# A convolution and attention kernel with its residual adds partly moved to accumulating DMAs, and its written-out orders made anew

## The chip, the cores and the metric

The kernel runs on one core of a Trainium2 chip. The metric is the time of one execution in microseconds of device time (us): lower is better. One execution of each kernel is also recorded by the hardware profiler; that gives the trace on which the readings rest. Five engines work side by side, each through its own instructions in order: TensorE (PE in the profile), VectorE (DVE), ScalarE (ACT), GpSimd (POOL) and SyncE (SP), which here only starts DMA transfers. They wait for one another through semaphores.

## The reference

The input is a residual stream x of 2048 tokens by 512 channels. Four layers run one after another: a long convolution, a local attention, the same convolution again, the same attention again, each on the layer-normalised stream and added back to it.

```python
def _A_ref(u, ...):                       # per channel d, states n = 0..127
    dt = jnp.exp(log_dt)[:, None]
    P = jnp.exp((dt * A)[:, :, None] * l[None, None, :])
    K = jnp.einsum("dn,dnl,dn->dl", Cc, P, dt * Bc).real      # kernel of 2048 taps
    y = irfft(rfft(u padded to 4096) * rfft(K padded))[:2048]
    return y + u * Dskip
def _B_ref(x, wqkv, wo):                  # 32 heads of 16, 8 taps, 2 tokens apart, causal
    q, k, v = (x @ wqkv) split
    logits = einsum(q, k at s, s-2, ..., s-14) / 4            # -1e9 ahead of token 0
    o = einsum(softmax(logits), v at the same tokens)
    return o @ wo
```

The convolution's kernel K is made once and used in both convolution layers.

## The kernel before

**Tiling.** The residual stream stays on the chip in one tile, X, 128 partitions by 16 "slots" of 512 channels in bfloat16: token 16p+j is in partition p, slot j. A slot is one 128x512 piece, and what follows in the attention is done by slot or by groups of four or eight slots.

**Stages.** There are five plans. The first makes the tables for K; the second finishes K (on PE, with sums evacuated by ScalarE or VectorE) and runs the first convolution as a two-step transform by matmuls; the third is the first attention (function b_layer), the fourth the second convolution (a_layer), the fifth the second attention. In the trace of before they end at about 60, 198, 308, 359 and 469 us.

**The order.** A layer's function doesn't issue its instructions directly. It puts operations on a list by `pl.op(engine, us, fn, *after)`, and where an operation can be done in several ways it puts all of them there with `pl.either(name, *ways)`. `Plan.run` then issues the operations in the order of one string of numbers per plan, ORDERS, which was written out by a planner offline; of a choice, those operations are issued whose numbers are in the string. `moved` (L317) is such a choice between a copy by ScalarE and one by VectorE. So a new ORDERS string can change both which engine does a step and what stands ahead of it on that engine. An engine runs its own instructions in this order whatever the others do; SP starts its transfers in it too, and if one must wait, all behind it wait.

**One attention**, with the lines named below:

- Statistics of the normalisation per slot (L166, VectorE), roots by Ln and Exp on ScalarE (L1401, L1402). The reciprocal deviations rs are needed for the earlier tokens too, which for some slots are one partition down: `shifted` (L1409), a small DMA from rs to rs by SP after a memset of partition 0 by POOL (L1420). Then rr, the products of the deviations of two tokens (L1422, VectorE), spread by ScalarE to RR (L1413), and ones written by POOL where no earlier token exists (L1419).
- Queries and keys by PE (L1436), evacuated to qT and kT by ScalarE or VectorE (L1441); the first columns of kT, shifted by a position, are filled by an SP transfer (L1446). Values into VX (L1456, L1467), with transfers that shift them (L1480).
- Logits: products on VectorE (L1501, 128x4096 or 128x2048), summed over a head's 16 channels on PE (L1512), copied back and turned (L1530, L1538, L1543), scaled by RR (L1581), masked by POOL (L1588).
- Softmax on 128x1024 tiles: a tree of maxima (L1562, VectorE), the maximum subtracted (L1624, VectorE), Exp (L1625, ScalarE); the sum either on PE (L1618) with Ln and Exp on ScalarE (L1599, L1603), or as a tree with a reciprocal on VectorE (L1593); the multiplication with it (L1627).
- Values: products on VectorE (L1640: 4096 columns, and 1024 or 512 in the last part), summed on PE (L1656, L1661) into po, evacuated by ScalarE (L1674, or L1676 straight into oT), and turned by an SP transposing transfer (L1679) into oT.
- The output projection of a slot: four matmuls by PE (L1719). Then the residual add in one of three ways: PE adds X by a matmul with the identity and ScalarE copies to X; or VectorE adds ps_o to X from PSUM (L1694); or ScalarE copies ps_o to oT (L1700) and VectorE adds oT to X (L1703). In the last attention the slot is then stored by SP (L1855).

The function `pv` (from L1630) builds the value part; `softmax`, just ahead of it, the subtraction and the sum; `out` the projection and the residual.

Of the kernel before, what the change touches and what calls it, by code (L numbers as in the profile page):

```python
# [10 lines left out]
ACT = mybir.ActivationFunctionType  # L11
# [33 lines left out]
STASH = ()  # L45

# [43 lines left out]
def make_consts(nc, const, C):  # L90
# [5 lines left out]
    for name in ("F1", "F1T"):  # L96
        C[name + "_h"] = nc.inline_tensor(_bf(fc[name]), name="c_" + name)
    todo = [("ident", _bf(np.eye(128)), BF), ("C2", _bf(fc["C2"]), BF), ("IC", _bf(fc["IC"]), BF),
            ("onesr", _bf(np.ones((1, 128))), BF)]
# [98 lines left out]
def load_params(nc, pp, prm):  # L198
# [1690 lines left out]
```

## Time and profile before

| what | value |
|---|---|
| median of 3 runs | 471.32 us (470.4 to 473.38) |
| profiled execution | 470.71 us, of which the traced span is 468.9 |
| granted TensorE clock | 0.999 |
| VectorE busy | 440.1 us (94%), 587 instructions |
| PE busy | 397.3 us (85%), 5255 matmuls |
| ScalarE busy | 347.1 us (74%) |
| POOL busy | 15.1 us (3%) |
| DMA | 49.34 MB in 110955 packets |
| DMAs started by POOL | none |

The span is the time from the first to the last traced instruction; the profiled execution's own time has some 1.8 us around it. Busy time counts an engine's instructions as the profiler saw them. A group of instructions is shown as line, engine, operation, tile written <- tiles read, shape, count, then busy time and mean duration (ns), then the time that the engine was idle just before them and what ended that. Durations of VectorE overlap a little with the next instruction's, so that the next starts some 0.07 us before the record's end.

### The profile page before, as it was taken

Reading aid. Unit: us, or ns where it says so; the run is one execution under the profiler, and the core shown is the slowest. Engines: PE = TensorE matmul, PEld = TensorE weight load, DVE = VectorE, ACT = ScalarE, POOL = GpSimd, SP = SyncE. Lnnn points to the kernel's source line nnn. Section 1 sums busy time; section 2 is a strip of 40 time slices with the busy share of each in tenths; the row PEclk is TensorE's granted clock in tenths of the full one; section 3 lists DMA queues with packets and bytes.
Section 4 is the critical chain, followed back from the end, with each engine's and each line's share of the span. In section 5 each row is a group of like instructions: output and inputs, shape, how many; then the busy total and the mean of one; then the engine's idle time right before and its main releaser. Section 6 shows DMA issues by size and latency. Waiting matters only on the chain. (4 is left out here: it accounts for less than half of the span.)

```text
span 468.9 us, 12383 instructions
## 1 busy us (share of the span) xinstructions
PE 397.3 (85%) x5255; PEld 244.0 (52%) x5255; DVE 440.1 (94%) x587; ACT 347.1 (74%) x546; POOL 15.1 (3%) x86
## 2 busy tenths in 40 slices
PE   1520688877999999899999979979998999998896
PEld 1410454544767768644466434666676445563353
DVE  6999999999999998589899999999996999999996
ACT  4999878895898878566786458999994668673341
POOL 0000000000000005000100000000000000100000
PEclk9999999999999999999999999999999999999999
DMA  8990036468379498521013221379937201113254
GB/s 234 189 344 22 3 93 140 56 102 173 103 139 202 78 150 175 139 49 62 36 46 106 51 45 30 91 223 182 194 73 98 49 7 49 60 46 78 46 135 113
DMA packets 110955, 49.34 MB, mean 105 GB/s; under 512 B 89019, under 2 KB 104124, under 8 KB 110644
## 3 DMA queue, kind: packets, MB, share of 16 engines
q1 hardware_dynamic: 110468, 48.16, 47.3%
q8 instruction: 41, 0.67, 0.6%
q10 hardware_dynamic: 432, 0.39, 0.3%
q14 instruction: 14, 0.11, 0.1%
HBM read 15.78 MB, written 8.13 MB: 51 GB/s over the span
## 5 line engine op out<-in xcount | busy, mean ns | idle before, releaser
L1640 DVE TENSOR_TENSOR prod<-VX,L 128x512 bf16<-128x512 bf16 (+2 forms) x72 | 75.7, 1101 | 0.3
L1501 DVE TENSOR_TENSOR prod<-qT,kT 128x4096 bf16<-128x4096 bf16 (+1 forms) x40 | 72.0, 1859 | 3.3 <-ACT kT L1441 2.9
L1436 PE MATMUL ps_qk<-U,wqk 128*128 128x512 bf16 x256 | 58.3, 379 | 1.7 <-ACT U L1361 1.1
L1656 PE MATMUL po<-prod,sb_ident 128*128 128x512 bf16 x224 | 52.4, 379 | 3.8 <-DVE prod L1640 3.6
L1436 PEld LDWEIGHTS <-wqk 128*128 128x128 bf16 x256 | 24.3, 97 | 33.8 <-issue 6.9
L1656 PEld LDWEIGHTS <-sb_ident 128*128 128x128 bf16 x224 | 21.6, 98 | 29.6 <-DVE prod L1640 3.6
L448 PE MATMUL ps_sum<-Ttab,sb_ident 128*128 128x512 bf16 x40 | 16.1, 403 | 19.9 <-DVE Ttab L409 19.2
L1719 PE MATMUL ps_o<-wo_t,oT 128*128 128x512 bf16 x128 | 32.7, 379 | 0.0
L865 ACT CAST Z<-ps_s 128x1024 bf16<-128x1024 f32 (+1 forms) x32 | 29.2, 978 | 4.2 <-PE ps_s L860 2.7
L1456 PE MATMUL ps_v<-wv,U 128*128 128x256 bf16 x256 | 31.6, 272 | 0.6 <-ACT VX L1467 0.3
L1467 ACT ACTIVATE VX<-ps_v,rs 128x256 bf16<-128x256 f32 x64 | 26.3, 473 | 5.6 <-PE ps_v L1456 5.0
L1456 PEld LDWEIGHTS <-U 128*128 128x128 bf16 x256 | 24.6, 97 | 8.4 <-issue 2.8
L473 DVE TENSOR_TENSOR Ttab<-Ttab,MPA 128x2048 bf16<-128x2048 bf16 (+2 forms) x20 | 28.1, 1429 | 0.0
L166 DVE BATCH_NORM_STATS2 ln_st_a<-X 128x6 f32<-128x512 bf16 x40 | 24.8, 680 | 3.1 <-ACT X L1001 2.9
L473 DVE TENSOR_TENSOR Y2tab<-Ttab,MPB 128x6144 bf16<-128x6144 bf16 (+1 forms) x13 | 27.2, 2120 | 0.0
L486 PE MATMUL psk<-Ttab 128*32 128x64 bf16 x1024 | 21.6, 201 | 4.0 <-DVE Ttab L473 4.0
L1674 ACT CAST ot<-po 128x1024 bf16<-128x1024 f32 x14 | 13.9, 1010 | 14.7 <-PE po L1656 11.7
L1441 ACT CAST kT<-ps_qk 128x512 bf16<-128x512 f32 x32 | 18.7, 584 | 7.6 <-PE ps_qk L1436 7.6
L489 PE MATMUL psk<-Y2tab,Ttab 128*32 128x48 bf16 x1024 | 21.2, 195 | 2.7 <-DVE Y2tab L473 1.7
L486 PEld LDWEIGHTS <-Ttab 128*32 128x32 bf16 x1024 | 19.3, 99 | 8.0 <-issue 7.0
L1441 ACT CAST qT<-ps_qk 128x512 bf16<-128x512 f32 x29 | 16.9, 587 | 8.3 <-PE ps_qk L1436 8.0
L453 ACT CAST Ttab<-ps_sum 128x1024 bf16<-128x1024 f32 (+1 forms) x24 | 20.5, 903 | 3.4 <-PE ps_sum L449 3.3
(233 smaller groups left out, 987.4 us busy)
## 6 DMA issues: line engine op xcount, KB each, us to landing
kt_scratch<-sp_k SPq DMA_DIRECT2D x16, 256.0 KB, 3.9
Kt<-kt_scratch SPq DMA_DIRECT2D x16, 256.0 KB, 5.3
X<-in_A_u_dram SPq DMA_DIRECT2D x8, 256.0 KB, 5.0
X<-in_A_u_dram SPq DMA_DIRECT2D x4, 512.0 KB, 5.0
out_dram<-X SPq DMA_DIRECT2D x16, 128.0 KB, 1.8
k_scratch<-KTq SPq DMA_DIRECT2D x7, 256.0 KB, 3.2
KT<-k_scratch SPq DMA_DIRECT2D x7, 256.0 KB, 3.9
VX<-VX SPq DMA_DIRECT2D x4, 448.0 KB, 3.7
```

The costliest lines, as they stand in the source:

```text
L166: self.nc.vector.bn_stats(self.st[:, j, part, :], X[:, :, j, a // 2:b // 2])
L473: nc.vector.tensor_tensor(d, src.to_broadcast([128, c, n, 2 * EYB]), mm, ALU.mult)
L486: nc.tensor.matmul(o.rearrange("e (s i) -> e s i", s=2), xs, T[:, 1:3, h, m // 2, :, t], start=(m == 0), stop=False, skip_group_check=True)
L865: nc.scalar.copy(box["Z", kind, dc][:, 0:n // 8, :, jq * 32:(jq + 1) * 32].rearrange("p g r k -> p r g k"), box.pop(("s1", kind, dc, jq))[ ...
L1436: nc.tensor.matmul(ps[:], wqk[:, ct, f0:f0 + 128], XT[:, ct // 2, 4 * s:4 * s + 4, ct % 2, :], start=(ct == 0), stop=(ct == 3))
L1441: copy((qT, kT)[which][fp][:, f2, o:o + 512], box.pop(("qk", which, fp, f2, s))[:])
L1456: nc.tensor.matmul(ps[:, jj].rearrange("p t h d -> p (t h d)"), XT[:, ct // 2, j + jj, ct % 2, :], wv[:, ct, fp * 256:(fp + 1) * 256], sta ...
L1467: nc.scalar.activation(out, ps, ACT.Identity, scale=r)
L1501: nc.vector.tensor_tensor(pr[:], windows(q, 0, 2), windows(kT[fp][:, a:a + n2, col(w):col(w) + 1024], -DIL * 128, 2), ALU.mult)
L1640: nc.vector.tensor_tensor(p2[:].rearrange("p w j t d h -> p w (j t) d h"), windows(v, -DIL * 256, taps), l.to_broadcast([128, taps, nj * 2 ...
L1656: nc.tensor.matmul(po[:, c:c + 512], ident[:], p2[:, t, k + j:k + j + 2].rearrange("p j t d h -> p (j t d h)"), start=first, stop=stop)
L1719: nc.tensor.matmul(ps, oT[:, ft // 2, o:o + 128], wo_t[:, ft, :], start=(ft == 0 and not res), stop=(ft == 3))
```

## The change

1. *Residual by DMA.* `out` gets a fourth way: ScalarE copies ps_o to oT (L1700 before), and POOL starts a DMA that reads oT and adds it to X where it lands. The new order takes it in the second attention for slots 0, 2, 3, 5 and 6.
2. *Shift by matmul.* `by_tensor` takes the place of the memset and the DMA of rs in both attentions: a float32 matmul with a shifted identity, `down`, into PSUM, and a copy (by ScalarE, in the new orders).
3. *Subtraction of the maximum by PE*, as another way: two matmuls add the logits and the negated maximum (with `minus`, the negated identity) in PSUM, and ScalarE takes Exp from there in two halves. The new order takes it once, in the second attention.
4. *Other ways of the last values*: `pv` is split into `pv` and `piece`, which offers five ways to evacuate and turn the values of slots 12 to 15. In the new orders the way taken is the one of the kernel before.
5. *More ways of smaller steps*: the extension of kT by a copy on ScalarE or VectorE instead of a DMA (taken once each in the first attention); statistics from sums of squares, `by_moments` (not taken).
6. *Constants*: `minus` (32 KB) and `down` (64 KB) are loaded in the first stage; two tiles, Drow and spread, move to a pool that is released later on.
7. *All five ORDERS strings are new.* Besides the above, some evacuations change engine. In the second plan three table sums and several evacuations move to VectorE and others to ScalarE, and some turns change between PE and DMA. In the second convolution some evacuations swap engines. In the second attention one softmax sum goes from PE and ScalarE to VectorE's tree with reciprocal, slots 1 and 7 go from adding out of PSUM to copying and adding, slot 13 the other way.

```diff
+SHIFT = True
-    todo = [("ident", _bf(np.eye(128)), BF), ("C2", ...
+    todo = [("ident", _bf(np.eye(128)), BF), ("minus", _bf(-np.eye(128)), BF), ("C2", ...
+            ("onesr", ...), ("down", np.eye(128, k=1, dtype=np.float32), F32)]
...
-            o = pl.op("G", 0.1, lambda: nc.gpsimd.memset(rs[0:1, 0:NV], 1.0))
-            o = pl.op("S", 0.5, shifted, o, *Rs.values(), lag=2.3)
+            def by_tensor():
+                def mm():
+                    ps = box["down"] = psA.tile([128, NV], F32, name="ps_down", tag="psA")
+                    nc.tensor.matmul(ps[:], C["down"][:], rs[:, NJ:NV + NJ], start=True, stop=True)
+                key = ("psA", "down")
+                return moved(pl, nc, ("down",), 0.2, 0.15, lambda copy: copy(rs[:, 0:NV], box.pop("down")[:]),
+                             pl.op("P", 0.2, mm, *Rs.values(), take=key), drop=key)
+            o = by_tensor() if SHIFT else by_dma()
...
-                Kx[fp, f2] = pl.op("S", 0.8, lambda: nc.sync.dma_start(...), Kd[fp, f2, 2], Kd[fp, f2, 3], lag=2.5)
+                Kx[fp, f2] = pl.either(("ahead", fp, f2), lambda: pl.op("S", 0.8, ahead(nc.sync.dma_start), ends, lag=2.5),
+                                       lambda: pl.op("A", 0.65, ahead(nc.scalar.copy), ends),
+                                       lambda: pl.op("V", 0.5, ahead(nc.vector.tensor_copy), ends))
...
+            def less_by_tensor(o):
...
+                        nc.tensor.matmul(ps[:], ident[:], Lf[:, ws], start=True, stop=False)
+                        nc.tensor.matmul(ps[:], C["minus"][:], x[2][:, 0, :].unsqueeze(1).to_broadcast([128, 4, 128]), start=False, stop=True)
...
+                        nc.scalar.activation(Lf[:, ws], box.pop(("less", h))[:], ACT.Exp, scale=DH ** -0.5)
...
+            o = pl.either(("less", fp, j0), lambda: less_by_vector(o), lambda: less_by_tensor(o))
...
+        def summed_taken(j):
+            nc.gpsimd.dma_start(X[:, :, j, :], spent(j), accum_op=ALU.add)
...
                     if res is None:
                         a = pl.op("A", 0.48, lambda: taken(j, box.pop(("o", j))[:]), a, drop=key)
+                        if slow:
+                            return pl.op("G", 1.2, lambda: summed_taken(j), a, lag=3.5)
                         return pl.op("V", 0.33, lambda: added_taken(j), a)
...
-                es.append(pl.either(("out", j), *ways[::-1] if qt in ADD_Q else ways, lambda: way(None)) if qt in VSTAT_Q else way(True))
+                es.append(pl.either(("out", j), *ways[::-1] if qt in ADD_Q else ways, lambda: way(None), lambda: way(None, True)) if qt in VSTAT_Q else way(True))
```

The numbers in `pl.op` are the planner's own figures for an operation; `Plan.run` doesn't use them.

More of the change, by code (lines that the diff above doesn't have):

```diff
@@ L1394, in by_sums, with by_moments, power, spread @@
                 return pl.op("A", 0.5, root, a)
+            def by_moments():
+                def power(j):
+                    nc.scalar.activation(halves(oT[:, j // 8, j % 8 * D:j % 8 * D + D]), X[:, :, j, :], ACT.Square, accum_out=rs[:, NV + j:NV + j + 1])
+                def spread():
+                    nc.vector.tensor_tensor(ln.mv[:, js, 0], nm[:, js], nm[:, js], ALU.mult)
+                    nc.vector.scalar_tensor_tensor(rs[:, NV + j0:NV + j1], rs[:, NV + j0:NV + j1], 1.0 / D, ln.mv[:, js, 0], ALU.mult, ALU.subtract)
+                def rooted():
+                    r = rs[:, NV + j0:NV + j1]
+                    nc.scalar.activation(nm[:, js], r, ACT.Ln, bias=eps[:, 0:1])
+                    nc.scalar.activation(r, nm[:, js], ACT.Exp, scale=-0.5)
+                key = ("psA", "sum", q)
+                a = pl.op("P", 0.9, sums, turned[q], Wd.get("k", []), take=key)
+                a = pl.op("V", 0.1, lambda: nc.vector.tensor_copy(nm[:, js], box.pop(("sum", q))[:]), a, drop=key)
+                b = [pl.op("A", 0.72, lambda j=j: power(j), ready) for j in range(j0, j1)]
+                return pl.op("A", 0.5, rooted, pl.op("V", 0.3, spread, a, b))
             def by_stats():
@@ L1630, in pv, with way, piece @@
         def pv(fp, j0, nj):
-            flat, np, taps = fp == 0 or j0 < 12, min(nj, 4), 2 if nj == 8 else 1
+            if nj > 2:
+                vs, last = piece(fp, j0, nj, True, None)
+            else:
+                before, vs, last = box["pv"], [], []
+                def way(flat, how):
+                    box["pv"] = before
+                    v, x = piece(fp, j0, nj, flat, how)
+                    vs.append(v)
+                    last.append(x)
+                    return Od[fp, j0]
+                o = pl.either(("piece", j0), lambda: way(False, "A"), lambda: way(False, "V"), lambda: way(True, "D"),
+                              lambda: way(True, "A"), lambda: way(True, "V"))
+                for k in range(j0, j0 + nj):
+                    Od[fp, k] = o
+            Od["last", fp, j0], box["pv"] = last, vs
+        def piece(fp, j0, nj, flat, how):
+            np, taps = min(nj, 4), 2 if nj == 8 else 1
             def part(w, first):
@@ L1678, in turn, with turn_mm, turn_back @@
             def turn(j):
-                nc.sync.dma_start(oT[:, fp, j * 256:(j + 4) * 256].rearrange("f (b p) -> f b p", p=128),
-                                  box.pop(("ot", fp, j))[:], transpose=True)
+                nc.sync.dma_start(oT[:, fp, j * 256:(j + np) * 256].rearrange("f (b p) -> f b p", p=128),
+                                  box.pop(("ot", fp, j))[:, 0:np * 256], transpose=True)
+            def turn_mm(j):
+                ot = box.pop(("ot", fp, j))
+                pt = box["pt", fp, j] = psO.tile([128, 4, 128], BF, name="pt_o", tag="psO")
+                for x in range(4):
+                    nc.tensor.transpose(pt[:, x, :], ot[:, x * 128:x * 128 + 128], ident[:])
+            def turn_back(copy, j):
+                copy(oT[:, fp, j * 256:(j + np) * 256].rearrange("f (b p) -> f b p", p=128), box.pop(("pt", fp, j))[:])
             os, vs = [], []
@@ L1719, in mm, with way @@
                         nc.tensor.matmul(ps, oT[:, ft // 2, o:o + 128], wo_t[:, ft, :], start=(ft == 0 and not res), stop=(ft == 3))
-                def way(res, j=j, key=key, mm=mm):
+                def way(res, slow=False, j=j, key=key, mm=mm):
                     if qt == 3:
```

52 lines of the change are left out of this document (37 added, 15 removed), and 120 rows, old and new, of the table ORDERS.

## The prediction

> **What bounds the kernel now.** I began with the page's busy totals, then cut the span into the five plans with the table by windows, and read three more views in the stages that the change touches: VectorE's waits, its groups of instructions, and the chain that ended last. The totals and the first stretch-by-stretch table:
>
> ```profile
> PE 397.3 (85%) x5255; PEld 244.0 (52%) x5255; DVE 440.1 (94%) x587; ACT 347.1 (74%) x546; POOL 15.1 (3%) x86
> ...
> 0.00:60.00 60.00, 22.10 (x588) 15.93 (x591) 54.51 (x97) 52.20 (x83) 0.90 (x11) 1.00 0.60 155
> 60.00:195.00 135.00, 120.28 (x2759) 83.00 (x2747) 130.38 (x146) 110.54 (x137) 7.47 (x13) 1.00 0.67 133
> 195.00:305.00 110.00, 104.03 (x739) 55.83 (x739) 103.77 (x140) 77.46 (x159) 3.35 (x31) 1.00 0.23 57
> 305.00:360.00 55.00, 50.90 (x505) 37.58 (x503) 48.06 (x78) 48.32 (x60) 0.10 (x1) 1.00 0.76 156
> 360.00:469.00 109.00, 100.02 (x690) 51.65 (x687) 103.41 (x130) 58.59 (x111) 3.31 (x30) 0.99 0.30 66
> ```
>
> Each row is a window: its length, then busy time of PE, weight loads, VectorE (DVE), ScalarE (ACT) and POOL, the granted clock, DMA. VectorE is filled in four of the five rows; only from 305 to 360, the second convolution, does PE lead (between 320 and 359 it is busy 37.82 of 39, VectorE 33.24). So a microsecond of VectorE in either attention should be worth nearly one, a microsecond of it in the second convolution little. VectorE's 26 us of idle time lie at the borders of stages:
>
> ```profile
> DVE prod L1501 <- ACT kT L1441: 2.9, 3, 1.3
> DVE ln_st_a L166 <- ACT X L1001: 2.9, 1, 2.9
> DVE X L1287 <- PE ps_y L1282: 2.7, 2, 1.4
> DVE pa L950 <- ACT sp_k L1059: 2.4, 2, 1.9
> DVE X L1694 <- PE ps_o L1719: 1.5, 5, 0.5
> ```
>
> (total, times, longest). The first attention begins with 1.33 us of waiting at 209.94 and 1.20 at 233.78 for keys that ScalarE had yet to evacuate; from 359 to the end VectorE almost never waits. The last part of the chain shows what ends the program:
>
> ```profile
> 442.12 2.21 DVE prod L1640
> 444.33 0.04 issue
> 444.38 1.89 PE po L1656 x8
> ...
> 462.79 2.60 PE ps_o L1719 x12
> 465.39 0.02 issue
> 465.41 0.69 DVE X L1694
> ```
>
> Up to 444.3 the chain is VectorE's products, and behind the last 4096-column product PE alone has 21.0 us without a hole. VectorE in the same stretch has 20.3 busy of 22. So here both must get shorter for the end to move.
>
> **The change, part by part.** The planned orders of the two kernels differ in which way each choice takes; I counted these per plan and priced them from the groups of the second attention:
>
> ```profile
> L1640 DVE TENSOR_TENSOR prod<-VX,L 128x4096 bf16<-128x4096 bf16 x12 | 27.1, 2287 | 0.0
> ...
> L1694 DVE TENSOR_TENSOR X<-ps_o,X 128x512 bf16<-128x512 f32 x11 | 7.6, 689 | 1.6 <-PE ps_o L1719 1.5
> ...
> L1624 DVE TENSOR_TENSOR L<-L,sm_m 128x1024 bf16<-128x1024 bf16 x4 | 2.8, 689 | 0.1
> ...
> L1703 DVE TENSOR_TENSOR X<-oT,X 128x512 bf16<-128x512 bf16 x5 | 2.1, 419 | 0.0
> ```
>
> (the last numbers: busy us, mean ns, idle before.) *Second attention.* Five residual adds go from VectorE to POOL's DMA: slots 0 and 3 save 2×0.69, slots 2, 5 and 6 save 3×0.42, 2.64 in all. Slots 1 and 7 become copy plus cheap add (−2×0.27), slot 13 the reverse (+0.27): −0.27. One subtraction of the maximum goes to PE (−0.69). Against that, one softmax denominator leaves PE and ScalarE for VectorE: a tree by L1562 (0.42+0.29+0.29) and a reciprocal like L1593's 0.95; by start-to-start pitch, a little under these durations, +1.63. The small rest: one key copy fewer net (−0.61). The sum is −2.6 by durations, and about −2.1 when each is counted by the pitch at which VectorE starts the next (some 0.07 under the duration). ScalarE gains five copies of 0.59 (L1700) and two Exp halves; it is busy 58.6 of 109, so I count them at nothing; if they queue ahead of an evacuation for PE they would cost their own 0.6 each, 1.2 at worst. Of the 2.1, 1.2 lie ahead of the last 4096-column product, which then ends at about 443.1. In the new order four slots' projections rather than two stand on PE ahead of that product's sums, so 2×0.86 (four matmuls each) less follows it, and the denominator's 0.45 has left PE: 19 us there instead of 21, while VectorE has 18.5 instead of 19.4 to do. Together **−2.1, bounds −0.9** (only the part ahead of the last product) **and −2.5**.
>
> *What that needs of the new transfers.* The trace has no DMA from POOL that reads and adds. Nearest rows: the 128 KB stores of L1855 land after 1.8 us, the transposes of L1679 after 3.1 (issue pitch 1.24), the 448 KB shifts after 3.7, and the slowest in the kernel after 9.6. On SP's queue, behind four transposes, stand the stores of slots 6 and 5, each waiting for its transfer, ahead of the transpose of slot 12; and the stores of 0 and 2 ahead of the last transpose. On this trace's clock, the transfers of 6 and 5 start at about 440.6 and 442, those of 0 and 2 at 444 to 445. The transpose of slot 12 can be issued at 447.7, needs 3.1, and PE uses it at 453: between 1 and 2 us of slack; the last has about 1. So a transfer from POOL may take some 5.7 to 7 us to landing for nothing; I take 3 to 4 (nearest: a transpose) and so 0. Its upper end, 9.6 and one behind another, is the slow rival below.
>
> *Does VectorE starve POOL?* POOL's memsets of L1588 (0.31 and 0.62 at 387.81 and 388.30) ran while VectorE's products had no gap, so POOL was not shut out by tensor-tensor work. The Trainium skill, "SBUF — State Buffer", section "SBUF: two separate sides", warns that a DMA issued from GpSimd can have its descriptors held up while VectorE runs a two-port mode; its section "Who interferes with whom" says that a two-input VectorE instruction contends only with a GpSimd instruction that reads SBUF. The memsets agree with the latter; if the former held for these products the transfers would come late, which is the slow rival. Beside it, "DMA: Bandwidth & Descriptors", section "Anatomy of one DMA — SWDGE (gpsimd) path", gives 2.0 us plus bytes by 436 GB/s, an estimate of 2.3 for 128 KB, that would leave the sum as it is; no run here shows that yet.
>
> *Shifting deviations* (L1409, L1420): a memset and an SP transfer per attention become one small matmul and a copy on ScalarE. Who waits is rr (L1422, 0.28), then RR (L1413); before, scaling (L1581) waited 0.23 for it once. The transfer's issue (0.74 at 216.48) leaves SP. Worth 0, with ends −0.3 and +0.6 (the copy queueing on ScalarE).
>
> *First attention.* VectorE's work is unchanged by count (two adds replaced, key copy and evacuations swapped, within 0.2). The order puts all 16 statistics (0.68 each) ahead of the first logits product, which covers the 1.33 hole, since keys come meanwhile; the 1.20 hole has no such cover. I take **−1.0, between −2.0 and 0**.
>
> *Tables and first convolution.* VectorE −0.6 in the first plan (a normalisation comes, two others go to ScalarE), +2.1 in the second: four table sums by VectorE, evacuations moved each way, half a value copy. Up to the last table product (before: 175.9) that nets **+0.4**. Behind it VectorE gets +1.2 and ScalarE +0.9, PE loses 0.35; there PE is at 10.97 of 11 from 176 to 187 and VectorE at 9.60, then VectorE has 2 gaps of 1.93 and 2.85 in the next 11 us, which hold 1.2: **0, ends −1 and +1**. The two constants added (32 and 64 KB) are read from DRAM at the start, where F1 lands some 20 us before its first use: 0, or 0.3 if they delay it.
>
> *Second convolution.* VectorE +1.7, ScalarE −1.4, PE unchanged, in a stage where PE has 37.82 of 39: **0, ±1**.
>
> Sum: −2.1 +0.4 +0 −1.0 +0 = −2.7, so 470.71 → 468.0 for the profiled execution. The median of the runs shown is 0.6 above it (471.32, of 470.4 to 473.38): **468.5**. The four unsettled terms together give 465.5 to 471.5.
>
> **Rivals.** *(a) The transfers are late: slower.* If POOL runs them one after another, each start to landing longer than 4 us, the stores that wait for them hold SP, and the transposes for slots 12 to 15 and 8 to 11 behind them come late; PE and VectorE then stand idle at the end. Four transfers from 440.6 at 5 us each end at 460.6 where about 453.2 was needed: +7.4, that is 476; at 6 us +11, 480. Four microseconds is the point from which it decides. For it: SP's order is fixed, and waits there hold everything behind. Against it: no transfer of this size in the trace pitches above 2 us. *(b) No gain: 471.5.* VectorE's work over the whole kernel is +1.0 us (−0.6 +2.1 +0 +1.7 −2.1); if the convolutions are not covered by PE, that takes 1.0 to 2.9 back, and a longer wait at a border takes the rest. For it: the added work lies in plans where VectorE has 130.4 of 135. *(c) More: 465.* The orders are all new, and the idle 1.9, 2.9 and 1.3+1.4 at the borders (second fence) could close too; half of that is 3.5 beyond my sum. Against it: those waits are for the chain at a border (last table, its inverse transform, its copy), not for order alone. *(d) The change does less than it says*: the ways for the last values are in the code but the planned orders take the old one, so nothing is to be had from them; I already count them at 0.
>
> **How the numbers follow.** A measurement here tells about 1% (4.7 us) from no change. Forecast 0.45 (467 to 470), (b) 0.22, (c) 0.16, (a) 0.17. Faster by over 1% means below 466.6: all of (c) and a little of the forecast, 0.21. Slower by over 1% means above 476.0: nearly all of (a) and little else, 0.16. The rest is within, 0.63. The range runs from 465 (the lower bounds of the sum, most of (c)) to 476.5 (the point where (a) begins to cost), leaving out about 2 in 10.
>
> **What would show it.** Right: VectorE's busy total near 441; the last 4096-column product about 3 us earlier; five POOL transfers landing in under 5 us; no idle on VectorE at the first logits product of the first attention; L1694 with fewer adds and without longer waits. Wrong: POOL transfers above 6 us and the transposes starting later than 449 and 454; PE idle above 1 us after the last products; VectorE busy above 443 with the second convolution longer than 55 us; or a new wait at the end for a store behind a transfer.

## The result, and the profile after

The changed kernel takes **473.71 us** (median of 18 runs; 473.68 without the one at 738.88) against 471.76 us for the kernel before, beside it on the same chip: a ratio of 1.004, with a 95% interval of 1.0025 to 1.0055. In a second measurement the ratio was 1.0015 (0.9999 to 1.0031). So the change costs between nothing and 2.6 us, most likely 1 to 2 us; forecast were 468.5 us, 3 us less than before. The trace that came with the result was taken at a granted clock of 0.753 and ran 738.88 us; it is left aside, and all lines of the changed kernel below are from the second measurement's profiled execution (472.06 us, span 470.3, clock 1.0).

First the totals, and the five windows that the prediction read (columns: window, length, PE, weight loads, VectorE, ScalarE, POOL, clock, DMA):

```profile
PE 394.7 (84%) x5270; PEld 242.4 (52%) x5270; DVE 441.1 (94%) x586; ACT 350.0 (74%) x555; POOL 21.1 (4%) x89
```

```profile
0.00:60.00 60.00, 21.40 (x644) 15.18 (x645) 54.69 (x97) 53.86 (x86) 0.96 (x12) 1.00 0.59 150
60.00:195.00 135.00, 117.89 (x2692) 80.82 (x2692) 130.64 (x146) 110.08 (x136) 7.41 (x13) 1.00 0.64 130
195.00:305.00 110.00, 103.42 (x743) 56.53 (x742) 103.29 (x136) 76.85 (x157) 3.31 (x30) 1.00 0.21 49
305.00:360.00 55.00, 50.79 (x500) 37.23 (x498) 48.63 (x81) 49.05 (x63) 0.00 (x0) 1.00 0.77 160
360.00:469.00 109.00, 101.17 (x698) 52.67 (x695) 103.86 (x130) 60.20 (x115) 9.46 (x35) 1.00 0.34 74
```

VectorE has 441.1 us of work where it had 440.1: the +1.0 that the prediction counted. The work was priced rightly; where its saving falls was not. The same fixed windows hardly differ, so I compared the two traces at marks, each the end or start of a named instruction:

| stage, from mark to mark | before | after | difference | forecast |
|---|---|---|---|---|
| start to the last table product | 175.98 | 176.11 | +0.13 | +0.4 |
| to the last X of the first convolution | 23.79 | 24.68 | +0.89 | 0 |
| to the last value product of the first attention | 100.29 | 100.76 | +0.47 | −1.0 |
| to the last X of the second convolution | 59.26 | 59.86 | +0.60 | 0 |
| to the end of the last 4096-column value product | 85.00 | 84.69 | −0.31 | −1.2 |
| to the last residual add | 21.79 | 20.96 | −0.83 | −0.9 |
| to the end of the span | 2.82 | 3.23 | +0.41 | 0 |
| sum | 468.93 | 470.29 | +1.36 | −2.7 |

The second attention gains, though less than forecast, and each stage ahead of it loses. The runs further on show how far one trace can be trusted, when only those are counted that have no stretch at half clock in the stage (last section). To the last X of the first convolution, the old order takes 23.3 to 23.9 us in eight traces and 25.2 in a ninth, the new one 24.7 to 25.7 in seven. The first attention takes 100.3 us in six traces before, and 100.75 in four after. To the last X of the second convolution, the old order takes 59.05 to 59.57 in five traces, the new one 59.86 and 60.12; so of its +0.60 a part may be scatter.

VectorE's waits in the changed kernel (total, times, longest):

```profile
DVE X L1288 <- PE ps_y L1283: 4.0, 2, 2.0
...
DVE X L1002 <- PE ps_y L998: 3.5, 2, 2.1
DVE prod L1535 <- ACT qT L1472: 3.1, 3, 1.8
DVE X L1783 <- PE ps_o L1811: 1.2, 5, 0.4
```

The wait at the first attention's logits was to close. There VectorE waited 2.53 us before (1.33 and 1.20, for kT) and waits 3.13 now (0.87, 0.46 and 1.80, for qT). The waits at the ends of the convolutions (L1288, L1002) grew. Groups of the second attention, from 361 us on (VectorE's, then POOL's):

```profile
L1783 DVE TENSOR_TENSOR X<-ps_o,X 128x512 bf16<-128x512 f32 x8 | 5.4, 690 | 1.2 <-PE ps_o L1811 1.2
...
L1660 DVE TENSOR_TENSOR L<-L,sm_m 128x1024 bf16<-128x1024 bf16 x3 | 2.1, 689 | 0.1
L1792 DVE TENSOR_TENSOR X<-oT,X 128x512 bf16<-128x512 bf16 x3 | 1.3, 417 | 0.0
```

```profile
L1795 POOL DMA_DIRECT2D X<-oT x5 | 6.2, 1325 | 13.6 <-DVE sm_m L1596 11.7 <-ACT oT L1789 1.8 <-issue 0.2
```

Eight adds from PSUM instead of 11, three cheap adds instead of five, and five transfers by POOL, each holding POOL for 1.2 to 1.7 us. They land after 3.3 to 5.4 us, median 3.5; the 3 to 4 that I took. The end of the chain is PE again, behind one transposing transfer of 5.80 us (issue included) where such a transfer takes 3.2:

```profile
438.20 3.18 PE po L1727 x14
450.95 5.80 DMA oT<-ot
463.75 2.60 PE ps_o L1811 x12
```

It cost PE 0.30 us of waiting at 456.80, no more.

### The profile page after: what moved, and what is told of

It reads as the page before. It is cut to its first block, busy times and chain, and to the rows that moved or that the text cites. A ratio compares the mean times of both kernels' runs of the same rounds, so it can differ in the third digit from the quotient of the medians.

```text
span 737.1 us, 12419 instructions
## 1 busy us (share of the span) xinstructions
PE 686.9 (93%) x5270; PEld 348.8 (47%) x5270; DVE 450.5 (61%) x586; ACT 358.9 (49%) x555; POOL 21.1 (3%) x89
## 4 chain that ended last, share of the span: by engine, by line
PE 90%; DVE 4%; SPq 3%; ACT 2%; DMA 1%; issue 1%; ACTq 0%
PE ps_qk L1467 14%; PE po L1727 12%; PE ps_v L1490 7%; PE ps_o L1811 7%; PE Lp L1546 4%; PE ps_s L861 3%; PE psk L487 2%; PE vp L975 2%; PE ps_y L998 2%; PE ps_sum L450 2%; PE vp L971 2%; PE ps_sum L449 2%; PE xp L881 2%; PE xp L884 2%; PE xp L883 2%; PE xp L882 2%
## 5 line engine op out<-in xcount | busy, mean ns | idle before, releaser
L1467 PE MATMUL ps_qk<-U,wqk 128*128 128x512 bf16 x256 | 105.9, 605 | 0.4 <-ACT U L1362 0.4
L1727 PE MATMUL po<-prod,sb_ident 128*128 128x512 bf16 x224 | 90.2, 582 | 1.1 <-ACT ot L1745 1.1
L1467 PEld LDWEIGHTS <-wqk 128*128 128x128 bf16 x256 | 33.9, 135 | 69.5 <-issue 67.1
L1727 PEld LDWEIGHTS <-sb_ident 128*128 128x128 bf16 x224 | 29.5, 133 | 55.2 <-issue 54.1
L1811 PE MATMUL ps_o<-wo_t,oT 128*128 128x512 bf16 x128 | 55.1, 579 | 0.0
L1490 PE MATMUL ps_v<-wv,U 128*128 128x256 bf16 x256 | 51.3, 385 | 0.1
L449 PE MATMUL ps_sum<-Ttab,sb_ident 128*128 128x512 bf16 x36 | 23.9, 664 | 20.4 <-DVE Ttab L410 19.7
L1501 ACT ACTIVATE VX<-ps_v,rs 128x256 bf16<-128x256 f32 x64 | 26.8, 472 | 28.2 <-PE ps_v L1490 28.2
L951 DVE TENSOR_TENSOR pa<-sp_u,sp_k 128x2048 bf16<-128x2048 bf16 x16 | 19.5, 1222 | 30.7 <-ACT sp_k L888 16.1
L1546 PE MATMUL Lp<-prod,sb_bones 128*32 128x512 bf16 x256 | 33.0, 566 | 0.0
L1237 DVE TENSOR_TENSOR pa<-xc,Kt 128x2048 bf16<-128x2048 bf16 x16 | 19.5, 1223 | 18.6 <-PE vp L1261 10.8
L971 PE MATMUL vp<-sb_IC,pa 128*128 128x256 bf16 x64 | 28.2, 448 | 0.0
L975 PE MATMUL vp<-sb_IC,pa 128*128 128x256 bf16 x64 | 28.2, 446 | 0.0
```

The lines of the kernel that those rows point to most:

```text
L449: self.nc.tensor.matmul(o, ident, a[:, i * n:i * n + n], start=True, stop=False)
L971: nc.tensor.matmul(o, pa[:, 0, sl], IC[:, 0, :], start=True, stop=False)
L975: nc.tensor.matmul(o, pa[:, 1, sl], IC[:, 2, :], start=False, stop=True)
L1467: nc.tensor.matmul(ps[:], wqk[:, ct, f0:f0 + 128], XT[:, ct // 2, 4 * s:4 * s + 4, ct % 2, :], start=(ct == 0), stop=(ct == 3))
L1490: nc.tensor.matmul(ps[:, jj].rearrange("p t h d -> p (t h d)"), XT[:, ct // 2, j + jj, ct % 2, :], wv[:, ct, fp * 256:(fp + 1) * 256], sta ...
L1546: nc.tensor.matmul(Lp[r0:r0 + 32, w // 4, :], bones[:, w % 4 + k, :], pr[:, k, f2 - a, hb * 512:(hb + 1) * 512], start=(n == 1 and k == 0) ...
```

## Which stages lose and which gain

Theories 1 to 3 were put against one another first: the loss is in the tables and convolutions (1), at the end of the program (2), or in the clock (3). The changed kernel and the kernel before ran once more unchanged.

> The changed kernel once more, for a trace at full clock: the one at hand was taken at a granted clock of 0.753 and runs 737 us. All theories expect some 2 us over the kernel before (473.7 against 471.8). Theory 1 (the loss is in the plans of tables and convolutions, where VectorE gets 0.4 + 1.2 + 1.7 us more): the second attention is some 2 us shorter than before in the trace, and the stages at 60-198 and 308-359 us together 4 to 5 us longer. Theory 2 (the loss is at the end, where stores wait for POOL's transfers): the stages up to 360 us are as long as before, and the stretch behind the last 4096-column product is 24 us or more instead of 21.7. Theory 3 (the clock): matmuls are longer in some stretch, with a granted clock under 1 there, and the other stretches are as before or shorter.

> The kernel before once more, for the granted clock of its executions and a second trace. Theory 3 (the changed kernel loses to the clock, 0.986 to 0.996 in most of its executions) expects 0.999 or 1.0 here in every one. Theories 1 and 2 expect the same mean clock in both kernels, about 0.99. Time 470.4 to 473.4.

The result: 473.08 us (ratio above) and 471.17 us. The table above is this trace. Theory 3 falls: both traces are at full clock (1.0 and 0.999) and differ by 1.4 to 1.6 us, and at like clocks the changed kernel is the slower one too: medians of 471.87 (3 executions) against 471.1 (28) at a mean clock of 0.9975 or more, and of 473.2 (15) against 472.1 (30) from 0.992 to 0.9975. How exact a ratio is can be seen from the kernel before, which against itself came out at 0.9981 (0.9963 to 0.9999): it can be off by some 0.002, or 0.9 us. Theory 1 is half right, theory 2 wrong: the stretch behind the last 4096-column product became shorter.

Plans 1, 2 and 4 (tables, both convolutions) have the same operations in both kernels, so their orders can be exchanged alone:

```diff
-ORDERS = [after1, after2, after3, after4, after5]   # the changed kernel
+ORDERS = [before1, before2, after3, before4, after5]   # convs_old; convs_new: the kernel before, the other way round
```

> The changed kernel with the orders of the kernel before in plans 1, 2 and 4 (tables, first and second convolution); both attentions as changed. Theory 1 expects the gain of the attentions alone, 2 to 3 us under the kernel before: 468.5 to 470. Theory 2 expects all of the loss still there: 473 to 475. Theory 3 expects 473 and a clock under 0.995 if the attentions bring the clock down, else as theory 1.

> The kernel before with the new orders in plans 1, 2 and 4 alone; both attentions and all constants as before. Theory 1 expects 4 to 5 us over the kernel before: 475.5 to 476.5. Theory 2 expects no difference, 471 to 472.5. Theory 3 expects a clock under 0.995 here if these plans bring it down, and some 2 us over.

Both are slower than the kernel before: 1.0037 (1.002 to 1.0054) and 1.0047 (1.0024 to 1.007). Theory 1 expected convs_old to be faster; it isn't, so the first attention loses too. Orders of neighbouring plans also seem to depend on each other: in the traces the same new first attention takes 101.21 us behind the old convolution and 100.75 behind the new one. I then put both versions of the attention into one file and exchanged the second attention alone: only it new (att2_new), or only it old (att2_old).

```diff
+# att2_new: plans 1 to 4 as before, the fifth (code and order) as changed
+def b_layer(*a):
+    return (b_layer_after if "bbbba"[Plan.turn] == "a" else b_layer_before)(*a)    # att2_old: "aaaab"
```

> Only the second attention (code and order) is the changed one; plans 1 to 4 are those of the kernel before. Theory 4 (each plan has its own balance: the second attention gains, the first three stages behind the tables lose): from the last X of the second convolution to the last residual add 105.6 us, as in the changed kernel's trace, instead of 106.8, and the last store 0.4 later behind it: 0.7 us under the kernel before, a ratio of 0.998 to 0.999. Rival (the gain in the second attention is only the new convolution handing over its slots in another order): 106.8 us or more from that point, a ratio of 1.000 to 1.006.

> The changed kernel with the second attention (code and order) of the kernel before; plans 1 to 4 as changed. Theory 4 (plans 1 to 4 lose, the second attention gains): last X of the second convolution at 361.4 us or later, as in the changed kernel, and from there 106.8 us plus a mismatch of up to 1.6 us where the old attention meets the new convolution's order of slots, as it was in the run with the new orders in plans 1, 2 and 4: 3.5 to 4.5 us over the kernel before, a ratio of 1.007 to 1.010. Rival (the second attention has no gain of its own): the changed kernel's time, 1.002 to 1.004.

> The kernel with only the second attention changed, once more: 0.995 to 0.998 of the kernel before. If its first ratio of 0.9963 was chance: 0.999 to 1.001.

Only the second attention new: **0.9963 (0.9943 to 0.9984)**, and again 0.9973 (0.9958 to 0.9989): 1.3 to 1.7 us faster than the kernel before, the best version of all. Only it old: 1.0057 (1.003 to 1.0085), some 2.7 us slower. The two add up to the result within the intervals. The mismatch of 1.6 us that I had added for att2_old is not there: its second attention takes 106.69 us from the convolution's last X to the last add, as before (106.79). I had it from the trace of convs_new, where a stretch of 3.41 us at half clock begins at 365.1 us, in the opening of that attention. With the new attention these are 105.2 in att2_new and 105.65 in the changed kernel. So by the times plans 1 to 4 lose some 2.7 us, and the second attention gives back 1.3 to 1.7; in the two traces of the table these are 2.1 and 1.1. Comparing att2_new with convs_old also prices the first attention's new order ahead of the *old* convolution: 3 us of time. (In the trace of convs_old the clock was halved for 6.8 us from 310 us on, so that it doesn't tell how much of that the order alone is.)

## What the accumulating transfers are worth

```diff
 def summed_taken(j):
-    nc.gpsimd.dma_start(X[:, :, j, :], spent(j), accum_op=ALU.add)
+    nc.vector.tensor_tensor(X[:, :, j, :], spent(j), X[:, :, j, :], ALU.add)
```

> The changed kernel with the five accumulating transfers replaced by adds of oT to X on VectorE (0.42 us each), at the same places of the order. Theory 4 (the transfers take VectorE work out of a stretch in which it and PE have no idle time): 1.0 to 1.7 us over the changed kernel, from five times 0.34 us of pitch. Rival (the transfers cost what they save, since one transposing transfer took 5.8 us instead of 3.1 beside them and stores wait for them): the same time as the changed kernel or up to 0.5 us less, and all transposing transfers at the end landing after 3.1 to 3.3 us.

> The kernel with only the second attention changed (ratio 0.9963 to the kernel before), with its five accumulating transfers replaced by adds on VectorE. Theory 4 (most of that attention's gain is the transfers): 1.0 to 1.7 us slower than with them, a ratio of 0.998 to 1.001 to the kernel before. Rival (the gain is the moved softmax and the order): 0.996 to 0.997 as with them.

In the changed kernel (add_by_vector): 1.0056 (1.0036 to 1.0076), some 0.8 to 1.9 us more than with the transfers; in the trace the second attention takes 106.83 instead of 105.65, +1.18. In att2_new: 0.9989 (0.9971 to 1.0007) instead of 0.9963 and 0.9973; in the trace 106.83 instead of 105.2, +1.6. Five times the pitch of 0.34 is 1.7. So the transfers are worth 1.2 to 1.6 of the 1.7 us of VectorE time that they free, and 106.83 is what the kernel before needs (106.79): *the rest of the second attention's change (the moved subtraction, the moved sum, the other copies, the order) nets nothing*.

The slow rival of the prediction was that a store waits on SP's queue for such a transfer, ahead of a transposing one. It does not come true with five; with two more it does:

```diff
 def added_taken(j):
+    if j in (1, 7):
+        return summed_taken(j)
     nc.vector.tensor_tensor(X[:, :, j, :], spent(j), X[:, :, j, :], ALU.add)
```

> The kernel with only the second attention changed, and slots 1 and 7 accumulated by POOL's transfers too: seven instead of five. Theory 4 (each add that leaves VectorE at the end is worth its pitch of 0.34 us, as long as no store waits ahead of a transposing transfer on SP): 0.3 to 0.7 us faster than with five, a ratio of 0.994 to 0.996. Rival (seven transfers of 1.2 us issue each come late, or the transposing transfer of slots 8 to 11 waits behind the store of slot 7): the same or up to 1 us slower than with five, 0.996 to 0.999.

The result: 1.003 (1.0011 to 1.0049), some 3 us slower than with five, of which the trace shows 2.0 (107.17 us from the convolution's last X to the last add, instead of 105.2). SP's queue at the end (start, duration, instructions), POOL's, and the matmul that waited:

```profile
449.99 1.71 SPq L1695 DMA_TRANSPOSE oT<-ot  x1
451.80 4.74 SPq L2365 DMA_DIRECT2D out_dram<-X  x3
456.63 1.38 SPq L1695 DMA_TRANSPOSE oT<-ot  x1
```

```profile
452.23 3.67 POOL L1742 DMA_DIRECT2D X<-oT  x3 [3.28 <-ACT oT L1734]
```

```profile
461.26 1.47 PE L1758 MATMUL ps_o<-wo_t,oT 128*128 128x512 bf16 x6 [2.06 <-DMA oT<-ot]
```

The last three transfers now start at 452.23 in a row. A store of a slot among them holds SP until 456.5, the transposing transfer behind it starts at 456.63, and PE waits 2.06 us for it. The transfers themselves land after 3.3 to 5.1 us, where with five they took 3.3 to 5.2; it is the place of their stores in SP's order that costs.

## What paces the opening of an attention

My prediction took VectorE's waits of 1.33 and 1.20 us in the first attention for time to be had. Two edits of the kernel *before* test that: more work for VectorE ahead of the first wait, or more for PE.

```diff
 def gather(j):
-    ln.gather(X, 0, j, j + 1)
+    for _ in range(2 if Plan.turn == 2 and j in (1, 3) else 1):     # stats_twice
+        ln.gather(X, 0, j, j + 1)
```

```diff
-for ct in range(4):
+for ct in list(range(4)) * (2 if twice else 1):       # qk_twice: two of the key projections
     nc.tensor.matmul(ps[:], wqk[:, ct, f0:f0 + 128], XT[...], start=(ct == 0), stop=(ct == 3))
```

> The kernel before, with the statistics of two slots taken twice in the first attention, ahead of its first logits product: 1.24 us more for VectorE by start-to-start pitch, the same result. Theory 5 (PE's projections pace the opening of the attention up to the product at 233.7 us; VectorE's idle 1.34 and 1.20 us are slack and filling them is worth nothing): the product that starts at 233.7 starts within 0.3 us of that, its wait or the one at 209.9 us shrinks by 1.2 us, and the time is unchanged within 0.3 us. Rival (VectorE paces it and the waits are bound to single evacuations): 1.2 us later from there on and 1.2 us slower.

> The kernel before, with the four matmuls of two key projections issued twice in the first attention ahead of its first logits product: eight matmuls of 0.216 us pitch, 1.73 us more for PE, the same result. Theory 5 (PE paces the opening): the product at 233.7 us starts 1.5 to 1.8 us later and the kernel is 1.5 to 1.8 us slower. Rival: PE has room there, and the product starts less than 0.6 us later.

In the first trace of the kernel before, the first logits product starts at 209.94 us, behind an evacuation of keys by ScalarE that had itself waited for PE:

```profile
209.32 0.58 ACT L1441 CAST kT<-ps_qk 128x512 bf16<-128x512 f32 x1 [0.28 <-PE ps_qk L1436]
```

Lines of VectorE's timeline: of the kernel before (its second trace), of stats_twice and of qk_twice, in each the first logits product and the one behind the second wait (start, duration, shape, idle before):

```profile
209.87 4.64 DVE L1501 TENSOR_TENSOR prod<-qT,kT 128x2048 bf16<-128x2048 bf16 x4 [1.34 <-ACT kT L1441]
...
233.71 4.50 DVE L1501 TENSOR_TENSOR prod<-qT,kT 128x4096 bf16<-128x4096 bf16 x2 [1.20 <-ACT kT L1441]
```

```profile
210.88 4.62 DVE L1506 TENSOR_TENSOR prod<-qT,kT 128x2048 bf16<-128x2048 bf16 x4
...
234.69 4.50 DVE L1506 TENSOR_TENSOR prod<-qT,kT 128x4096 bf16<-128x4096 bf16 x2 [1.20 <-ACT kT L1446]
```

```profile
213.05 4.63 DVE L1502 TENSOR_TENSOR prod<-qT,kT 128x2048 bf16<-128x2048 bf16 x4 [3.06 <-ACT kT L1442]
...
236.88 4.50 DVE L1502 TENSOR_TENSOR prod<-qT,kT 128x4096 bf16<-128x4096 bf16 x2 [1.20 <-ACT kT L1442]
```

Counted from the convolution's last X, the second of these products starts after 34.01 us in the kernel before, 34.02 with 1.24 us more VectorE work (the wait of 1.34 has gone, the time is the same: ratio 0.999, 0.997 to 1.0011), and 35.73 with 1.73 us more PE work (+1.72). Theory 5 holds in the traces: **PE's projections pace the opening, and VectorE's waits there are slack**. In time, qk_twice cost less than expected, 1.0013 (0.9995 to 1.0032): its trace has 1.72 us more at the end of the attention and 0.9 to 1.1 more at the end of the second convolution (against either trace of the kernel before), so the following stage gave some back.

In the changed kernel the same two products are

```profile
211.83 4.64 DVE L1535 TENSOR_TENSOR prod<-qT,kT 128x2048 bf16<-128x2048 bf16 x4 [0.87 <-ACT qT L1472]
...
235.00 4.49 DVE L1535 TENSOR_TENSOR prod<-qT,kT 128x4096 bf16<-128x4096 bf16 x2 [1.80 <-ACT qT L1472]
```

They start 11.04 and 34.21 us after the convolution's last X, instead of 10.17 and 34.01. In the second attention the second of them starts after 33.18 us before and 33.15 after the change, although the first logits product there moved 0.95 us forward. Neither opening became shorter.

## What the smaller parts are worth

**The shift by matmul**, undone in both attentions: the matmul becomes the memset, the copy becomes the SP transfer, at the same places of the order.

```diff
-ps = box["down"] = psA.tile([128, NV], F32, name="ps_down", tag="psA")
-nc.tensor.matmul(ps[:], C["down"][:], rs[:, NJ:NV + NJ], start=True, stop=True)
+nc.gpsimd.memset(rs[0:1, 0:NV], 1.0)
...
-lambda copy: copy(rs[:, 0:NV], box.pop("down")[:])
+lambda copy: shifted()
```

> The changed kernel with the deviations shifted by memset and SP transfer again, in both attentions. Theory 4 gives the shift no part in the result: within 0.3 us of the changed kernel, as the pair products rr come about 2 us later but are wanted only some 10 us later. Rival (ScalarE's and PE's added work at the opening of the attentions delays the keys and queries that VectorE waits for there, 0.87 + 0.46 + 1.80 us in the first one): 0.5 to 1 us less than the changed kernel, with shorter waits at the first logits products.

1.0035 (1.0016 to 1.0053), no different from the changed kernel's own ratios; from the convolution's last X to the last value product it takes 100.9 us instead of 100.8. As forecast: 0.

**The end of the first convolution.** One of VectorE's added evacuations there goes back to ScalarE:

```diff
-ORDERS[1] = "... 701 ..."      # KTq from psk(7, 1) by VectorE
+ORDERS[1] = "... 700 ..."      # by ScalarE
```

> The changed kernel with one evacuation at the end of the table work (KTq from psk, at 178 us, 0.68 us on VectorE) back on ScalarE, in the same place of the order. Theory 4a (the first convolution's end is longer by 0.9 us because VectorE has more to evacuate there): its last X 0.5 to 0.6 us earlier than 200.8, and the time 0.5 us less than the changed kernel's. Rival 4b (PE and ScalarE pace that end and VectorE waits there anyway): last X within 0.2 us of 200.8, the time unchanged.

The convolution's end: 24.70 us behind the last table product instead of 24.68; 1.0026 (1.0006 to 1.0046). So giving the step back to ScalarE gains nothing, as 4b said. That VectorE's added work is hidden there this run alone doesn't show, for two things changed in it: PE waits for ScalarE's KTu and starts the sums ps_u at 180.50 us instead of 179.92, and a hole in PE's work is gone that the changed kernel has. PE's idle time in this stage grew from 2.42 us (kernel before) to 3.23. The hole, 0.51 us of it, lies *inside* a group of equal matmuls and has no releaser:

```profile
180.15 0.56 PE L1034 MATMUL ps_u<-KTu,sb_F 128*128 128x32 bf16 x16
181.23 0.54 PE L1034 MATMUL ps_u<-KTu,sb_F 128*128 128x32 bf16 x15 [0.51 <-issue]
```

In seven traces with the new order and full clock in this stage the hole is 0.51 to 1.35 us long, and the stage less its hole is 24.2 to 24.4 us in every one. So the hole comes through in full: it is some 0.5 of the +0.89. Another 0.27 may be PE's wait at vp (L971), 0.50 us for VectorE's products where it was 0.23 for ScalarE; the rest is open.

**The second convolution.** At its start PE waits 2.59 us for the normalised U, the last three of which ScalarE makes in a row. I gave one of them to VectorE (u_one, run twice), then two (u_two), and last took a cast of VT from VectorE (vt_act), each a number in an order string:

```diff
-ORDERS[2] = "... 780 ... 778"    # U of slots 9 and 8 by ScalarE
+ORDERS[2] = "... 780 ... 777"    # u_one: slot 8 by VectorE;  u_two: "... 779 ... 777"
-ORDERS[3] = "... 71 ..."         # VT by VectorE
+ORDERS[3] = "... 66 ..."         # vt_act: by ScalarE
```

> The changed kernel with the normalised input U of one slot (slot 8, the last of three that ScalarE makes in a row at 309.9 to 312.2 us, while PE waits 2.59 us for them) made by VectorE instead, in the same place of the order. Theory 6 (the second convolution starts later because ScalarE's last three U end last): PE's wait shrinks by 0.6 to 0.8 us, and the convolution's end comes 0.4 to 0.8 us earlier. Rival (VectorE, whose casts of Z then start 0.35 us later, or the transposing transfers later on pace the convolution): its end moves less than 0.2 us.

> The changed kernel with the U of slot 8 made by VectorE, once more. In the first trace the granted clock was 0.81 to 0.91 from 310 to 322 us. Theory 6 (PE's wait for ScalarE's last U paces the second convolution) expects, in a trace without such a dip between 305 and 365 us, 59.0 to 59.5 us from the last product of the first attention to the last X of the convolution, instead of 59.9. Rival: 59.7 us or more.

> The changed kernel with the U of slots 8 and 9 both made by VectorE: ScalarE's row of three becomes one. Theory 6: PE's wait of 2.59 us falls to 1.3 to 1.7 us and the same stretch to 58.6 to 59.4 us; the time 0.5 to 1.0 us under the changed kernel's, a ratio of 1.000 to 1.002 against the kernel before. Rival (VectorE, with 0.7 us more ahead of its casts of Z, paces it): 59.7 us or more, and the changed kernel's ratio of 1.002 to 1.004 or above.

> The changed kernel with one cast of VT in the second convolution (1.22 us on VectorE at 326.3 us) back on ScalarE, in the same place of the order. Theory 7 (VectorE, with 1.1 us more to do and 1.1 us idle of 31 between 310 and 341 us, paces that stretch): the convolution's last X 0.5 to 1.1 us earlier against the last product of the first attention, 59.3 us or less instead of 59.9, and the time 0.5 to 1.0 us less. Rival (the product at 333.7 us waits 0.64 us for Kt's transfer already, so the wait grows by what VectorE saves): 59.7 us or more, that wait at 1.2 us or more, and the time unchanged.

Measured: 1.0043 (1.0028 to 1.0058), 1.0044 (1.0013 to 1.0074), 1.0071 (1.0045 to 1.0098) and 1.0034 (1.0014 to 1.0053): none is clearly faster than the changed kernel (1.0015 and 1.004); u_two's ratio is the highest, but its interval still meets the changed kernel's. PE's wait did shrink, to 1.64 us with one U on VectorE, but with two only to 2.09, where 1.3 to 1.7 were expected. In all four traces the clock was at half for 3.41 us, starting between 313.1 and 314.9, so their stage lengths, 60.3 to 60.9 us, can't be set against 59.86. Three other traces of the same order have such a stretch from 315.0 to 316.5 us on (add_by_vector, att2_old, shift_by_dma) and take 60.4 to 60.8: theory 6, that this wait paces the convolution, is not borne out. For theory 7 vt_act's waits answer. It freed 1.1 us of VectorE ahead of a product that waited 0.6 us for a transfer in the changed kernel; now that wait is

```profile
DVE pa L1182 <- DMA Kt<-kt_scratch: 1.5, 1, 1.5
```

so what VectorE saved went into waiting for Kt, as the rival said. Why that transfer is late stands in SP's queue, first of the kernel before and then of the changed one:

```profile
315.95 6.61 SPq L1195 DMA_TRANSPOSE zt<-Z  x4
322.96 0.32 SPq L1295 DMA_DIRECT2D Kt<-kt_scratch  x1
323.39 2.65 SPq L1195 DMA_TRANSPOSE zt<-Z  x2
326.09 1.14 SPq L1295 DMA_DIRECT2D Kt<-kt_scratch  x2
```

```profile
314.43 14.06 SPq L1196 DMA_TRANSPOSE zt<-Z  x9
328.54 1.53 SPq L1296 DMA_DIRECT2D Kt<-kt_scratch  x3
```

The new order issues nine transposing transfers in a row, 14 us, ahead of loads of Kt that stood between them before; the product at 333.67 waits 0.64 us for the first. Moving these loads forward was not tried, so what of the stage's 0.60 us they account for stays open.

## Why the prediction was wrong

**The work of VectorE** (+1.0 over the kernel, by counts and rows): right, 441.1 against 440.1. (The five terms that rival (b) lists for it add up to +1.1.)

**The transfers in the second attention** (0 as long as they land within 5.7 to 7 us): right. They land after 3.3 to 5.4 and free 1.2 to 1.6 us. The row of the nearest transfer (3.1) was a good price; the 2.3 estimated beside it is under the fastest. That VectorE's products held POOL up doesn't show: three of the five issues took 1.20 us in the midst of them, the others 1.32 and 1.71; but no run has such an issue without them. The sentence of the Trainium skill ("SBUF — State Buffer", "Who interferes with whom") that a two-input VectorE instruction disturbs only a GpSimd instruction that reads SBUF agrees with that as far as it goes.

**The second attention's −2.1**: half right. Behind the last large product −0.83 came of −0.9 (−1.2 to −1.3 in att2_new). Ahead of it −0.31 came of −1.2. The step that failed is "so a microsecond of VectorE in either attention should be worth nearly one". The evacuation that left VectorE (0.6; one of queries, by the rows, and not of keys) lies in the opening, where PE paces, and brought nothing; of the moved subtraction's 0.6, 0.28 us came through behind it (51.54 us from the product at 33.15 us to the end of the last large one, instead of 51.82 from 33.18). The sum itself has a slip that the −2.1 doesn't share: its "−2.6 by durations" takes the added softmax sum by pitch; by durations throughout it is −2.3.

**The first attention's −1.0**: wrong, +0.47 came. The failed step is "the order puts all 16 statistics ahead of the first logits product, which covers the 1.33 hole, since keys come meanwhile". The kernel before already has 15 of the 16 there, so the order moves one, 0.6 us, and the keys did not come meanwhile: a wait of 0.87 us is left, that product starts 0.87 later, and the wait at the second mark grew from 1.20 to 1.80. stats_twice shows that even full cover is worth nothing: the wait is for PE, which from 202 to 233 us has no hole of its own. Of the +0.47, 0.20 are there when the second of the products starts. The other 0.27 come behind it, where VectorE has the same work as before (65.8 us) and idles 0.74 us instead of 0.47; why stays open. The line that I quoted, "DVE prod L1501 <- ACT kT L1441", names ScalarE; ScalarE itself was waiting for PE's ps_qk.

**The first convolution's end, 0 with ends −1 and +1**: +0.89, within its bounds. Some 0.5 of it is the hole in PE's own work, for which the prediction has no term; whether VectorE's added work was hidden, as it said, is not settled.

**The second convolution, 0**: +0.60, within its ±1. The cover that I named, PE at 37.82 of 39, is an average over 320 to 359; between 310 and 341 VectorE idled 2.1 us of 31 before and 0.9 after. One thing that is shown to hold it up in the changed kernel is SP's queue, 0.64 us at 333.67, which I had not walked through for this plan; its share of the +0.60 is open.

**The rivals**: (a), late transfers, did not come with five; with seven no transfer took longer, but a store that waits for one held SP ahead of a transpose, as (a) had it. (b), no gain because the convolutions take it back, was the nearest, and the time lies 2 us above it, as the first attention lost too. (c) and the closing of the waits at the borders did not happen: they grew (4.0 and 3.5 us at L1288 and L1002). (d) is how I counted it. The 471.5 that the prediction gives as the upper end of its four unsettled terms is less than their upper bounds add up to, which is 472.8.

## What to carry to other kernels

Before counting an engine's idle time as a gain, follow its releaser back one engine further: a wait for an evacuation that itself waits for PE is PE's time, and filling it moves nothing. An accumulating transfer was worth most of the add that it freed where VectorE was the bound, as long as no store that waited for it stood on a queue ahead of a transfer that PE needed. When all orders are made anew, exchange them plan by plan: here one plan of five held the whole gain, and with that one alone the kernel is 1.3 to 1.7 us faster than before.

## What the runs showed of the hardware that I had not expected

*The clock falls for one stretch at a time.* The clock records of the traces hold stretches at half clock in the midst of full clock, most of 3.41 us, some of 6.83, and in two traces one of 37.55 from 16.1 us on. In the window of one, in u_one (clock is the column behind POOL's):

```profile
311.00:319.00 8.00, 5.91 (x62) 5.13 (x62) 7.04 (x11) 5.84 (x8) 0.00 (x0) 0.79 0.93 220
```

Executions differ in how many they have. Of the kernel before, 30 executions with a mean clock of 0.9975 or more have a median of 471.07 us, 34 with less than 0.987 one of 473.1; a good part of the scatter between runs is this, and a stage in one trace can be 1 to 2 us off by it. The Trainium skill ("TensorE: Matmul & The Clock Gate", "What's actually happening") names a free-running window of 3413 ns, and the length agrees. It has the clock fall after a whole idle window; in u_one the longest time that PE was idle in the 10 us ahead of the stretch was 1.65 us.

*A hole inside a group of short matmuls.* The hole in ps_u at 181 us was 0.51 to 1.50 us long in nine traces with the new second plan, and each time it ended 2.3 to 2.8 us after a 16 KB instruction transfer had started. With the old order there was none at this place, nor in ktq_act, though such a transfer started there too, at 178.88. That PE had run out of instructions is the obvious reading; it was not tested.

*The end of the span.* Behind the last residual add the changed kernel and most of its variants need 3.1 to 3.2 us to the end, the kernel before, att2_new and add_by_vector 2.8, with the same last store; why is open.
